# Attention and a gated feed-forward on one core: the mask and the identity loaded from SyncE's row, with the hand-written order of chunks 0 to 2 rewritten

## The chip, the core and the metric

The kernel runs on one core of a Trainium2 chip. TensorE (PE; its weight loads are listed as PEld), VectorE (DVE), ScalarE (ACT), GpSimd (POOL) and SyncE (SP) each run their own row of instructions in order and wait for each other by semaphores. The metric is the device time of one execution, in microseconds (us).

## The reference, cut to what matters

```python
# q, k, v: (4, 8, 768, 64); block 32, window 16
k_sum = k.reshape(B, H, 24, 32, D).max(axis=3)
v_sum = v.reshape(B, H, 24, 32, D).mean(axis=3)
scores_l = where(|i - j| < 16, q @ k.T / 8, -1e9)
scores_s = q @ k_sum.T / 8 + log(32)
a = softmax(concat(scores_l, scores_s))
x = a @ concat(v, v_sum)                      # heads side by side: (4, 768, 512)
h = relu(x @ w_in)                            # 512 -> 1024
gate = sigmoid(conv over 3 neighbours in the sequence, per feature, of h)
out = (h * gate) @ w_out                      # 1024 -> 512
```

Everything is float32.

## The kernel before, in words

The batch is worked off in 8 **chunks** of half a sequence (384 positions), and a chunk in 4 **head pairs**, so pairs are numbered n = 0 to 31. In a pair the scores of 6 query blocks of 64 are taken against 96 near keys and 24 block maxima.

The steps have short names, and a string `ORDER` lists them, in the order in which they are written, for chunks 0 to 2; each engine works off its own steps in that order. From chunk 3 on loops write the order, and they are not touched. The names, with n a pair, c a chunk, u a group of 128 of the 1024 features, fc one of the 8 parts of a weight:

- loads on SP: `R` transposed keys (400 KB), `Q` queries (192 KB), `T` transposed values (384 KB), `I`, `O` the raw words of w_in, w_out (512 KB a part), `V`, `K`, `M`, `C` values, keys, value means and convolution weights;
- attention: `ks` block maxima of the keys (DVE), `win` and `kb` copies of the near keys and of the maxima into one tile (POOL, or DVE with the letter v or for pair 0), `qk` scores (24 matmuls on PE), `mx` mask and row maximum (DVE, reads the mask), `ex` exponential (ACT), `sm`, `rc`, `nr` the row sum, its reciprocal and the scaling (ACT, DVE, POOL), `tr` transposes (PE, read the identity), `cp` the copy of these out of PSUM, `vs`, `pv`, `vm`, `vb` the means of the values, `av` the product with the values (PE), `xh`, `xl` its upper and lower part (ACT, DVE); `ed` copies two columns of the chunk before into a new chunk's xh and xl (DVE, L439);
- weights are put together from 64-bit words: `z` (ACT), `lo`, `st` (DVE, L179 and L185), then `hi` (ACT) and `wl` (POOL, L205), with i for w_in and o for w_out, and `locw`, `stcw` for the convolution weights;
- feed-forward: `f` first product of unit u, 4 parts of 3 matmuls (PE, L458), `re` relu, `ta`, `cv` the convolution, `th`, `mu` the gate (`mu` is DVE's L513 and is the last to read the PSUM tile of its unit), `gh`, `gl` upper and lower part, `g` second product (PE, L545);
- `w` n is n matmuls on a zero tile (L150): 12 stand ahead of the list (`WARM`).

Three PSUM tiles hold the units of the first product, so the first part of unit u can start when `mu` of unit u - 3 is done: `f0.3.0` after `mu0.0`, `f0.7.0` after `mu0.4`, `f1.1.0` after `mu0.6`, `f1.4.0` after `mu1.1`. The scores of pair n wait for all `mx` of pair n - 1. A text such as `sto0<nr5.1p` makes a step wait for another one, here DVE's `sto0` for POOL's `nr5.1`; in the code these are called shared port.

The mask (180 KB) and the identity (64 KB) are loaded ahead of the list, on ACT's own row, while SP begins with `R0 R1 Q0 R2`:

```python
        w(WARM)
        nc.scalar.dma_start(mask, mask8)
        nc.scalar.dma_start(ident, ident_in)
        for text in ORDER.split():
            run(text)
```

Of the kernel before, what the change touches and what calls it, by code (L numbers as in the profile page):

```python
# [48 lines left out]
mx0.0.1 kb4 Q3 mx0.0.2 zi1 kb2 mx0.1.0 loi1<kb2 ex0.0.2 mx0.1.1 ex0.1.0 sti1 V0 zi0 mx0.1.2 loi0
T1 ex0.0.1 w13 qk1 ex0.1.1 sti0 ex0.1.2 V1 mx1.0.0 win5<sti0 hii1 mx1.0.1 sm0 win3 hii0 mx1.0.2  # L50
rc0 Q4 mx1.1.0 ex1.0.1 nr0.0p mx1.1.1 T2 ex1.0.2 mx1.1.2 ex1.1.1 vs0 nr0.1p w9 tr0 ex1.1.0 qk2
ex1.1.2 wli0 ks3 T3 ex1.0.0 pv0 cp0a mx2.0.0 vm0 win6 w1 tr1 mx2.0.1 sm1 zi2 mx2.0.2 C rc1 kb3
ex2.0.1 mx2.1.0 kb5 V2 mx2.1.1 cp1a loi2<kb5 zi6 mx2.1.2 sti2 w6 qk3 ex2.0.2 I5 nr1.0v ex2.1.0
ex2.1.2 loi6 tr2 I4 vb0v ex2.1.1 ex2.0.0 sti6 av0 sm2 Q5 cp2a mx3.0.0 nr1.1p<sti6 rc2 mx3.0.1
hii2 vs1 V3 nr2.0p hii6 w1 tr3 mx3.0.2 cp3a pv1 nr2.1p T11 mx3.1.0 ex3.0.0 tr4 vm1v mx3.1.1 xh0
vb1 mx3.1.2 cp4a I3 xl0 w1 qk4 ex3.0.2 I7 wli2 vs2 ex3.1.0 av1 ex3.0.1 R8 mx4.0.0 ex3.1.1 vs3
wli1 pv2 ex3.1.2 tr5 vm2 sm3 mx4.0.1 xh1 pv3 f0.0.0 M4 mx4.0.2 ex4.0.1 win7 rc3 mx4.1.0 ex4.0.0
xl1 f0.1.0 vb2 zcw vm3 mx4.1.1 f0.0.1 cp5a mx4.1.2 Q6 ex4.1.1 locw<vb2 f0.2.0 nr3.0v ex4.1.2 O0
av2 stcw zi5 loi5 nr3.1v ex4.0.2 f0.1.1 sti5 xh2 tr6 zi4 wli6v qk5 cp6a loi4 ex4.1.0 tr7 sti4
hii5 mx5.0.0 vb3<sti4 sm4 xl2 cp7a hii4 mx5.0.1 rc4 kb7 w4 av3 mx5.0.2 ex5.0.0 wli4 mx5.1.0  # L60
ex5.0.1 vs11 f0.1.2 xh3 f0.0.2 ex5.0.2 mx5.1.1 nr4.0p O1 xl3 zi3 f0.2.1 Q7 mx5.1.2 ex5.1.0
loi3<nr4.0p f0.1.3 Q8 ex5.1.2 sti3 f0.0.3 M6 zi7 M7 kb6v tr8 loi7 re0.0 pv11 K8 f0.2.2 sti7 hii3
V4 ta0.0a ks8 f0.2.3 nr4.1p<sti7 M5 re0.1 qk6 wli3 cv0.0.0 cp8a ta0.1a tr9 cv0.0.2 re0.2 cv0.1.0
wli5 ex5.1.1 th0.0 mx6.0.0 cv0.1.2 sm5 cp9a hii7p mx6.0.1 th0.1 mu0.0 ta0.2a loo0<hii7p w9
f0.3.0 mx6.0.2 zo0 gh0.0p<loo0 rc5 mu0.1 f0.3.1 nr5.0p zo1 O2 mx6.1.0 cv0.2.0 f0.4.0 gh0.1 R10
gl0.0 mx6.1.1 tr10 ex6.0.2 ed4 f0.3.2 mx6.1.2 ex6.1.0 cv0.2.2 nr5.1p ex6.0.1 qk7 cp10v th0.2
sto0<nr5.1p ex6.1.2 f0.4.1 ex6.0.0 mx7.0.0 f0.3.3 loo1 ex6.1.1 f0.4.2 kb8v O4 sto1 vm11 re0.3
tr11 V5 hio0 mx7.0.1 gl0.1<sto1 f0.4.3 mu0.2 V6 sm6 ta0.3a av4 mx7.0.2 Q9 re0.4v wlo0 gh0.2 R9
rc6 mx7.1.0 ex7.0.0 f0.5.0 cv0.3.0 xh4 mx7.1.1 f0.5.1 nr6.0p cp11a cv0.3.2 ta0.4a g0.0 mx7.1.2
wli7 xl4 zo2 f0.5.2 cv0.4.0 ex7.0.1 tr12 ex7.1.1 ks10 nr6.1p f0.5.3 th0.3 qk8 cp12a loo2<nr6.1p  # L70
hio1 mu0.3 gl0.2<loo2 O3 tr13 ex7.1.2 cv0.4.2 K9 f0.6.0 re0.5 sto2<gl0.2 av5 th0.4 ta0.5a
mx8.0.0 wlo1<sto2 mu0.4 f0.6.1 gh0.3 mx8.0.1 ex7.0.2 f0.7.0 cv0.5.0 ex7.1.0 gl0.3 f0.6.2 mx8.0.2
zo4 cv0.5.2 f0.7.1 mx8.1.0 sm7 xh5 loo4 f0.6.3 th0.5 rc7 sto4 T8 f0.7.2 hio2 V7 mx8.1.1 g0.1
nr7.1p<sto4 cp13v re0.6 K10 ex8.0.0 mu0.5 f0.7.3 nr7.0p ta0.6a xl5 f1.0.0 ex8.1.1 wlo2 ks9 tr14
zo3 av6 cp14a cv0.6.0 kb9 hio4 g0.2 mx8.1.2 loo3<kb9 ex8.1.2 cv0.6.2 gh0.5p<loo3 O6 f1.0.1 re0.7
V8 sto3<gh0.5p tr15 th0.6 qk9 xh6 mu0.6 gl0.5<sto3 hio3 xl6 f1.1.0 cp15a vs8 wlo3 f1.0.2 ta0.7a
ex8.1.0 av7 mx9.0.0 O5 cv0.7.0 gh0.6 wlo4 Q10 ex8.0.1 f1.1.1 mx9.0.1 cv0.7.2 xh7 g0.3 mx9.0.2
th0.7 xl7 gl0.6 f1.1.2 ex8.0.2 mx9.1.0 mu0.7 zo6 f1.0.3 loo6 gh0.4 f1.2.0 mx9.1.1 T9 sto6 re1.0
f1.1.3 V9 ta1.0a kb10v pv8 mx9.1.2 f1.2.1 loo5 sm8 zo5 cv1.0.0 gl0.4<loo5 qk10 re1.1 rc8 O7
cv1.0.2 f1.2.2 ex9.1.2 Q11 sto5 th1.0 g0.4 vm8 nr8.0p<sto5 mu1.0 hio5 M8 f1.2.3 vs9 ta1.1a R11  # L80
wlo5 f1.3.0 gh0.7 Q12 tr16 cv1.1.0 hio6 M11 pv9 f1.3.1 re1.2 K11 nr8.1p cv1.1.2 g0.5 ex9.1.0 T10
mx10.0.0 cp16v gl0.7 th1.1 Q14 f1.3.2 mx10.0.1 ex9.0.0 mu1.1 tr17 vm9 ta1.2a f1.3.3 mx10.0.2 M9
gh1.0v cp17a f1.4.0 K12 cv1.2.0 wlo6<gh1.0v ex9.0.1 V11 av8 mx10.1.0 ex9.1.1 cv1.2.2 ex9.0.2
gl1.0 mx10.1.1 f1.4.1 th1.2 ks11 sm9 g0.6 re1.3 mu1.2 xh8 R17 f1.4.2 zo7 rc9 mx10.1.2 K13 f1.5.0
loo7 ex10.1.1 sto7 T17 f1.4.3 ta1.3a xl8 f1.5.1 kb11<sto7 ex10.0.2 nr9.0p hio7 cv1.3.0 qk11
ex10.1.2 wlo7 cv1.3.2 f1.5.2 K14 vs10 th1.3 tr18 f1.5.3 re1.4 nr9.1p mu1.3 ex10.1.0 T16 g0.7
mx11.0.0 cp18a V12 gh1.1p mx11.0.1 f1.6.0 M12 ob0 gh1.2v<gh1.1p gh1.3v tr19 mx11.0.2 kb12<gh1.3v
f1.6.1 mx11.1.0 ex10.0.1 re1.5v pv10 g1.0 ex10.0.0 gl1.3v f1.6.2 mx11.1.1 sm10p<gl1.3v ta1.4a
cp19v g1.1 ex11.0.0 rc10 cv1.4.0 ex11.1.1 nr10.0p f1.6.3 mx11.1.2 vm10 cv1.4.2 ex11.0.2 g1.2 M10
gl1.2 ex11.1.2 Q13 tr20 V10 qk12 nr10.1p ta1.5a ex11.1.0 g1.3 kb13 ex11.0.1 mx12.0.0 K15 gl1.1  # L90
cv1.5.0 th1.4 av9 mx12.0.1 cp20a mu1.4 sm11 g1.4 mx12.0.2 xh9 rc11 re1.6 xl9 tr21 g1.5 ta1.6a
cv1.5.2 cp21a mx12.1.0 f1.7.0 mx12.1.1 ex12.1.0 nr11.0v g1.6 th1.5 cv1.6.0 gh1.4p<nr11.0v
ex12.0.1 f1.7.1 kb14 cv1.6.2 tr22 g1.7 mu1.5 th1.6 mx12.1.2 gh1.5 av10 vs16 ex12.1.2 ex12.0.2
qk13 nr11.1v T18 cp22a xh10v gl1.5<nr11.1v M13 ob1 f2.0.0 mu1.6 R16 f1.7.2 mx13.0.0 K16 ex12.0.0
xl10 f2.1.0 Q17 ex12.1.1 mx13.0.1 vs17 f1.7.3 tr23 re1.7 mx13.0.2 g2.0 gl1.4v cp23a sm12v f2.0.1
ta1.7v pv17 rc12 g2.1 mx13.1.0 vm17 cv1.7.0 ex13.0.1 av11 kb15v gh1.6v nr12.0v g2.2 cv1.7.2
gl1.6<nr12.0v xh11 M15 ex13.1.0 Q15 mx13.1.1 f2.1.1 xl11 ex13.0.2 Q16 f2.0.2 nr12.1v th1.7 V15
mx13.1.2 f2.1.2 mu1.7 V13 f2.0.3 gh1.7p f2.2.0 re2.0 gl1.7 qk14 ex13.0.0 ex13.1.2 pv16 ex13.1.1
tr24 K17 f2.1.3 ta2.0a mx14.0.0 vm16v g2.3 sm13 mx14.0.1 re2.1 cp24v f2.2.1 ta2.1a mx14.0.2
cv2.0.0 tr25 ex14.0.2 rc13 g2.4 cv2.0.2 ex14.0.0 nr13.0p cp25a cv2.1.0 f2.2.2 th2.0 nr13.1p  # L100
mx14.1.0 g2.5 ex14.0.1 ks16 tr26 mx14.1.1 g2.6 cv2.1.2 ex14.1.1 mu2.0 av12 cp26a ex14.1.0
# [697 lines left out]
```

## Time and profile before

| | us |
|---|---|
| median of 3 runs | 378.69 (377.99 to 379.32) |
| the profiled execution, its own time | 379.11 |
| its span in the trace | 377.3 |
| PE busy | 368.1 |
| DVE busy | 255.2 |
| ACT busy | 236.6 |
| POOL busy | 140.7 |

The zero matmuls count as busy PE time. The views are the page, the windows (busy time of each engine in a stretch), the chain that ended last, the timeline of an engine, and the groups of instructions by line. Starts in the timeline of one engine can be closer together than the durations say, since instructions overlap by some tenths of a microsecond.

### The profile page before, as it was taken

How to read it: one execution, taken by the hardware profiler on the slowest of the kernel's cores; microseconds unless marked ns; L12 is line 12 of the kernel's file. 1: busy time of each engine (PE TensorE's matmuls, PEld its weight loads, DVE VectorE, ACT ScalarE, POOL GpSimd, SP SyncE). 2: the span in 40 equal slices, each digit the busy share in tenths (PEclk: the TensorE clock that was granted, in tenths of full speed). 3: DMA queues.
4: the chain of work that ended last, by engine and by line, in shares of the span. 5: the costliest groups of instructions: out<-in, count | busy, mean ns of one | idle time of the engine just before them, and what ended most of it. 6: DMA issues, size and time to landing. Idle time of an engine off the chain costs nothing.

```text
span 377.3 us, 8779 instructions
## 1 busy us (share of the span) xinstructions
PE 368.1 (98%) x3140; PEld 311.9 (83%) x3144; DVE 255.2 (68%) x801; ACT 236.6 (63%) x766; POOL 140.7 (37%) x182
## 2 busy tenths in 40 slices
...
GB/s 294 378 342 309 208 247 215 261 298 256 199 210 133 51 253 239 152 319 130 96 74 112 99 129 96 132 132 59 85 36 2 30 31 22 6 30 28 28 57 56
DMA packets 26859, 55.01 MB, mean 146 GB/s; under 512 B 3072, under 2 KB 11456, under 8 KB 26816
## 3 DMA queue, kind: packets, MB, share of 16 engines
...
q8 instruction: 25, 0.41, 0.5%
q14 instruction: 18, 0.15, 0.1%
...
## 4 chain that ended last, share of the span: by engine, by line
PE 84%; DVE 6%; POOL 5%; DMA 1%; issue 1%; ACT 1%; DVEq 0%; POOLq 0%; ACTq 0%
PE f L545 35%; PE f L458 32%; PE xp L416 6%; PE pt L402 5%; PE pq L345 5%; POOL win_lo L205 2%; PE pw L150 1%; DMA va<-vm 1%; POOL a L394 1%; DVE wu_i L185 1%; DVE a L359 1%; DVE wl_i L179 1%; POOL kw L300 1%; DVE t L513 0%; DVE t L495 0%
## 5 line engine op out<-in xcount | busy, mean ns | idle before, releaser
L526 POOL TENSOR_TENSOR glo<-t,ghi 128x383 fp32r<-128x383 f32 (+1 forms) x61 | 61.6, 1017 | 119.3 <-ACT ghi L523 93.4
L458 PE MATMUL f<-xh,win_hi 128*128 128x386 f32 (+1 forms) x256 | 91.6, 358 | 0.4 <-DVE t L513 0.2
L458 PE MATMUL f<-xh,win_lo 128*128 128x386 f32 (+1 forms) x256 | 86.4, 338 | 0.0
L458 PE MATMUL f<-xl,win_hi 128*128 128x386 f32 (+1 forms) x256 | 86.4, 338 | 0.0
L495 DVE SCALAR_TENSOR_TENSOR t<-f,cw,t 128x382 f32<-128x382 f32 (+3 forms) x128 | 78.4, 615 | 11.3 <-ACT t L484 8.8
L374 ACT ACTIVATE a<-a,nm 128x120 f32<-128x120 f32 x192 | 73.7, 386 | 10.8 <-DVE nm L359 9.1
L545 PE MATMUL f<-wout_hi,ghi 128*128 128x512 f32 x192 | 76.9, 401 | 0.0
L545 PE MATMUL f<-wout_lo,ghi 128*128 128x512 f32 x192 | 75.3, 392 | 0.0
L545 PE MATMUL f<-wout_hi,glo 128*128 128x512 f32 x192 | 75.0, 391 | 0.0
L458 PEld LDWEIGHTS f<-xh,win_hi 128*128 128x128 f32 x256 | 48.2, 188 | 6.3 <-DVE t L513 2.1
L506 ACT ACTIVATE t<-t 128x383 f32<-128x383 f32 (+1 forms) x64 | 32.4, 523 | 30.2 <-DVE t L495 29.6
L359 DVE CUSTOM_DVE_ANT_0 a<-pq,mask 128x120 f32<-128x120 f32 x192 | 45.8, 274 | 6.8 <-PE pt L402 3.8
L473 ACT ACTIVATE f<-f 128x386 f32<-128x386 f32 (+1 forms) x60 | 28.5, 475 | 34.6 <-PE f L458 34.4
L394 POOL TENSOR_TENSOR a<-a,sm 128x360 f32<-128x360 f32 x53 | 41.0, 789 | 24.7 <-DVE sm L390 8.6
L458 PEld LDWEIGHTS f<-xl,win_hi 128*128 128x128 f32 x256 | 48.3, 189 | 1.9
L458 PEld LDWEIGHTS f<-xh,win_lo 128*128 128x128 f32 x256 | 48.1, 188 | 0.0
L513 DVE SCALAR_TENSOR_TENSOR t<-t,f 128x383 f32<-128x383 f32 (+1 forms) x64 | 34.2, 551 | 15.9 <-ACT t L506 15.9
L486 DVE TENSOR_SCALAR t<-f,cw 128x385 f32<-128x385 f32 (+1 forms) x36 | 22.2, 616 | 31.6 <-ACT f L473 29.8
L545 PEld LDWEIGHTS f<-wout_hi,glo 128*128 128x128 f32 x192 | 36.0, 188 | 8.0
L545 PEld LDWEIGHTS f<-wout_hi,ghi 128*128 128x128 f32 x192 | 36.1, 188 | 5.8 <-issue 0.3
L545 PEld LDWEIGHTS f<-wout_lo,ghi 128*128 128x128 f32 x192 | 36.2, 188 | 4.5
L407 ACT COPY aT<-pt 120x384 f32<-120x384 f32 x56 | 26.5, 472 | 17.5 <-PE pt L402 17.4
...
## 6 DMA issues: line engine op xcount, KB each, us to landing
...
```

Of the source, the lines that this page charges most:

```text
L359: nc.vector.tensor_tensor_reduce(aa[n, h][:, i, :], pq[n][h][:, i * NK : (i + 1) * NK], mask[:, {(0, 0): 0, (1, 2): 2}.get((hf, i), 1), :] ...
L374: nc.scalar.activation(a, a, AF.Exp, bias=nm[n][:, h, i : i + 1], scale=-1.0, accum_out=sm[n][:, h, i : i + 1],)
L394: return engine[e].tensor_tensor(a, a, sm[n][:, h, :].unsqueeze(2).to_broadcast([P, 3, NK]), ALU.mult)
L407: return copy(aT[j][:NK, :], pt.pop(j)[:NK, : 3 * P])
L416: nc.tensor.matmul(xp[n][r, blk * QB : (blk + 1) * QB], v[:NK, blk, r], a[h][:NK, blk * QB : (blk + 1) * QB], start=True, stop=True,)
L458: nc.tensor.matmul(f1ps[c, u][:, :n], w[:, u, cc, :], x[:, cc, :n], start=(cc == 0 and m == 0), stop=(cc == NCC - 1 and m == 2),)
L473: nc.scalar.activation(h, h, AF.Relu)
L495: nc.vector.scalar_tensor_tensor(t[:, i0:i1], f1ps[c, u][:, hf + k - 1 + i0 : hf + k - 1 + i1], cw[:, u, k : k + 1], t[:, i0:i1], ALU.mult ...
L506: nc.scalar.activation(t, t, AF.Tanh, scale=0.5)
L513: return nc.vector.scalar_tensor_tensor(t, t, 1.0, h, ALU.add, ALU.mult)
L526: return engine[e].tensor_tensor(gate_rows("lo", c, u), conv.pop((c, u)), gate_rows("hi", c, u).bitcast(F32), ALU.subtract,)
L545: nc.tensor.matmul(f2ps[b, st], g[:, fc, ss], w[:, fc, :], start=(fc == 0 and m == 0), stop=(fc == NFC - 1 and m == 2),)
```

## The change

ACT's two loads ahead of the list are gone. A new step `X` issues them from SP: `X0`, the mask, stands as the fourth load behind `R0`, `Q0` and `R1`, and `X1`, the identity, as the tenth. The whole list of chunks 0 to 2 is written anew: which step stands where, and for some steps which engine does them.

```diff
-R0 R1 Q0 R2 I1 I0 Q1 ks0 R3 win0 T0 kb0 ks1 win1 Q2 qk0 I2 kb1 ks2 win2 I6 win4 mx0.0.0 ex0.0.0
...
+R0 Q0 R1 X0 I0 Q1 ks0 I1 win0 kb0 T0 qk0 R2 ks1 X1 Q2 kb1 R3 mx0.0.0 win4 V0 ex0.0.0 mx0.0.1
...
     def locw():
-        lower("cw", NFC * 3)
+        return lower("cw", NFC * 3)
...
+        "X": lambda i: nc.sync.dma_start(*((mask, mask8), (ident, ident_in))[i]),
...
         w(WARM)
-        nc.scalar.dma_start(mask, mask8)
-        nc.scalar.dma_start(ident, ident_in)
         for text in ORDER.split():
             run(text)
```

In the new list `locw` waits for nothing (before: `locw<vb2`), and POOL's `vb3` waits for it. On DVE's row ahead of `mu1.1` these steps stand now that didn't before (from POOL or ACT, or from behind `mu1.1`): `cp5`, `gh0.0`, `gl0.2`, `kb4`, `kb5`, `kb9`, `ks11`, `nr2.1`, `vb2`, `wli2`, `wli5`, `wlo4`; and these no longer stand there: `cp10`, `cp13`, `cp16`, `kb6`, `kb8`, `kb10`, two `mx10`, `nr1.0`, `nr3.0`, `nr3.1`, `re0.4`, `vb0`, `vm1`.

The order that comes of it, at three places. First, SP's row at the start of the program; kT are keys, raw_a words of w_in, raw_b there words of w_in or values. Before:

```order
L260 DMA kT_92<-kT 128x800
L260 DMA kT_94<-kT 128x800
L273 DMA q_96<-qT 128x384
L260 DMA kT_98<-kT 128x800
L223 DMA raw_a<-w_in 128x1024 x2
L273 DMA q_102<-qT 128x384
L260 DMA kT_106<-kT 128x800
L268 DMA raw_b<-vT 128x768
```

and now:

```order
L261 DMA kT_90<-kT 128x800
L274 DMA q_92<-qT 128x384
L261 DMA kT_94<-kT 128x800
L568 DMA mask<-mask 128x360
L224 DMA raw_a<-w_in 128x1024
L274 DMA q_98<-qT 128x384
L224 DMA raw_a<-w_in 128x1024
L269 DMA raw_b<-vT 128x768
L261 DMA kT_121<-kT 128x800
L568 DMA ident<-ident 128x128
```

The keys of pair 2 (kT_98 before, kT_121 now) went from the fourth load to the ninth. Second, DVE's row at its start, before:

```order
L145 MEMSET idle 128x256
L294 TENSOR_REDUCE ks_104<-kT_92 128x24
L300 COPY kw_108<-kT_92 128x6x96
L294 TENSOR_REDUCE ks_112<-kT_94 128x24
L294 TENSOR_REDUCE ks_134<-kT_98 128x24
L359 ISA a_0_142,nm_141<-pq_0_118,mask 128x120
```

and now:

```order
L146 MEMSET idle 128x256
L295 TENSOR_REDUCE ks_100<-kT_90 128x24
L301 COPY kw_103<-kT_90 128x6x96
L295 TENSOR_REDUCE ks_123<-kT_94 128x24
L360 ISA a_0_133,nm_132<-pq_0_107,mask 128x120
```

The maxima of pair 2 (`ks2`) no longer stand ahead of the first masked scores (`mx0.0.0`). Third, the two copies of `ed4` on DVE, which stood behind `mu0.1`, in the middle of the convolution of unit 2 (t_2), before:

```order
L495 SCALAR_TENSOR_TENSOR t_2_713<-f_0_2_500,cw,t_2_713 128x382
L359 ISA a_1_745,nm_702<-pq_1_673,mask 128x120
L359 ISA nm_702 128x1
L439 CAST xh_764<-xh_397 128x4x2
L439 CAST xl_765<-xl_398 128x4x2
```

and now:

```order
L186 SCALAR_TENSOR_TENSOR wu_i_612<-wu_i_612,wl_i_607 128x512
L440 CAST xh_629<-xh_367 128x4x2
L440 CAST xl_630<-xl_368 128x4x2
L180 TENSOR_SCALAR wl_i_636<-raw_a 128x512
L311 TENSOR_REDUCE vs_639<-vt_425 128x24
L186 SCALAR_TENSOR_TENSOR wu_i_622<-wu_i_622,wl_i_636 128x512
```

They stand now between `sti4` (wu_i_612) and `loi3` (wl_i_636), ahead of `mu0.0`. On POOL `nr4.0` must be done before `sti4` starts, and the next POOL step, `nr4.1`, waits for `loi3`.

## Rows read from the trace of the kernel before

**Rows 1.** Windows: stretch, its length, then busy us (instructions) of PE, PEld, DVE, ACT and POOL, PE's granted clock, DMA share, GB/s.

```profile
60.00:70.00 10.00, 10.00 (x114) 8.60 (x113) 9.87 (x30) 9.34 (x26) 7.55 (x9) 1.00 0.74 257
70.00:80.00 10.00, 10.00 (x95) 8.79 (x95) 9.72 (x30) 9.75 (x33) 7.04 (x7) 1.00 0.92 297
```

**Rows 2.** The chain that ended last, its pieces at 56 us (start, us, what): `mu0.4` and the first matmul of unit 7, `f0.7.0`.

```profile
56.13 0.48 DVE t L513
...
56.65 0.45 PE f L458
```

**Rows 3.** Timeline (start, us): three times DVE's `mu` and the first matmul of the unit that waits for its tile, `mu0.0` and `f0.3.0`, `mu0.6` and `f1.1.0`, `mu1.1` and `f1.4.0`; at 76.87 `f1.3.3`, which stands ahead of `f1.4.0` here.

```profile
40.88 0.55 DVE L513 SCALAR_TENSOR_TENSOR t<-t,f 128x383 f32<-128x383 f32 x1
...
41.49 0.44 PE L458 MATMUL f<-xh,win_hi 128*128 128x384 f32 x1 [0.19 <-DVE t L513]
...
64.22 0.55 DVE L513 SCALAR_TENSOR_TENSOR t<-t,f 128x383 f32<-128x383 f32 x1
...
64.97 0.45 PE L458 MATMUL f<-xh,win_hi 128*128 128x386 f32 x1
...
76.09 0.55 DVE L513 SCALAR_TENSOR_TENSOR t<-t,f 128x385 f32<-128x385 f32 x1
...
76.87 0.42 PE L458 MATMUL f<-xh,win_hi 128*128 128x386 f32 x1
...
77.48 0.34 PE L458 MATMUL f<-xh,win_hi 128*128 128x386 f32 x1
```

**Rows 4.** Timeline of the start (start, us; ACTq is an issue on ACT's row): the two loads, the 12 zero matmuls, `ks0`, `qk0`, `ks2` and `mx0.0.0`.

```profile
0.72 0.41 ACTq L603 DMA_DIRECT2D mask<-mask  x1
...
1.16 0.45 ACTq L604 DMA_DIRECT2D ident<-ident  x1
...
1.17 5.30 PE L150 MATMUL pw<-idle 128*128 128x512 bf16 x12 [1.17 <-DVE idle L145]
...
4.76 0.95 DVE L294 TENSOR_REDUCE ks<-kT 128x24 f32<-128x768 f32 x1 [3.65 <-DMA kT<-kT]
...
6.58 0.99 PE L345 MATMUL pq<-kw,q 64*64 64x120 f32 x24
...
7.46 0.95 DVE L294 TENSOR_REDUCE ks<-kT 128x24 f32<-128x768 f32 x1 [0.53 <-DMA kT<-kT]
...
8.34 0.27 DVE L359 CUSTOM_DVE_ANT_0 a<-pq,mask 128x120 f32<-128x120 f32 x1
```

**Rows 5.** Windows of the start, columns as in rows 1 (the last is GB/s of the loads).

```profile
0.00:3.00 3.00, 1.83 (x5) 0.74 (x6) 0.27 (x1) 1.28 (x1) 0.19 (x4) 1.00 0.29 54
3.00:4.00 1.00, 1.00 (x4) 0.31 (x3) 0.00 (x0) 0.00 (x0) 0.00 (x0) 1.00 0.97 378
4.00:5.00 1.00, 1.00 (x4) 0.32 (x3) 0.24 (x1) 0.00 (x0) 0.00 (x0) 1.00 1.06 409
5.00:11.00 6.00, 5.77 (x47) 2.60 (x49) 5.40 (x19) 2.35 (x9) 3.15 (x7) 1.00 1.04 412
```

**Rows 6.** Line L439, all four runs of each copy of `ed` (ns: least, median, most), and then the timeline around `ed4`, of DVE and of POOL.

```profile
L439 DVE CAST xh<-xh x4: 172/297/760, 43.5 to 274.8; 128x8 fp32r<-128x8 f32 x4
L439 DVE CAST xl<-xl x4: 159/172/832, 44.1 to 274.7; 128x8 fp32r<-128x8 f32 x4
...
43.47 0.76 DVE L439 CAST xh<-xh 128x8 fp32r<-128x8 f32 x1
44.14 0.83 DVE L439 CAST xl<-xl 128x8 fp32r<-128x8 f32 x1
...
43.18 1.02 POOL L526 TENSOR_TENSOR glo<-t,ghi 128x383 fp32r<-128x383 f32 x1
44.16 0.79 POOL L394 TENSOR_TENSOR a<-a,sm 128x360 f32<-128x360 f32 x1
```

**Rows 7.** Timeline around `locw` (L179, 24 elements a partition), the like-sized `stcw` (L185), and POOL's `vb2`.

```profile
27.27 0.66 DVE L179 TENSOR_SCALAR wl_cw<-cw_words 128x24 uint32<-128x24 uint32 x1
...
28.28 0.17 DVE L185 SCALAR_TENSOR_TENSOR cw<-cw,wl_cw 128x24 uint32<-128x24 uint32 x1
...
27.07 0.82 POOL L332 COPY va<-vm 24x768 f32<-24x768 f32 x1
```

**Rows 8.** Groups by line and shape on DVE up to 80 us (count, busy us, mean ns of one): `ks`, `cp`, `nr`, `wl`, `kb`, `re`, `vb`, `gh`, `vm`.

```profile
L294 DVE TENSOR_REDUCE ks<-kT 128x24 f32<-128x768 f32 x8 | 7.6, 947 | 4.2 <-DMA kT<-kT 4.2
...
L407 DVE COPY aT<-pt 120x384 f32<-120x384 f32 x3 | 1.6, 548 | 0.0
L394 DVE TENSOR_TENSOR a<-a,sm 128x360 f32<-128x360 f32 x3 | 1.6, 528 | 0.0
...
L205 DVE TENSOR_TENSOR win_lo<-wu_i,win_hi 128x512 fp32r<-128x512 f32 x1 | 0.7, 699 | 0.0
L304 DVE COPY kw<-ks 128x144 f32<-128x144 f32 x3 | 0.7, 226 | 0.0
...
L475 DVE TENSOR_SCALAR f<-f 128x384 f32<-128x384 f32 x1 | 0.6, 559 | 0.0
L332 DVE COPY va<-vm 24x768 f32<-24x768 f32 x1 | 0.6, 553 | 0.0
...
L523 DVE CAST ghi<-t 128x385 fp32r<-128x385 f32 x1 | 0.4, 356 | 0.0
L328 DVE TENSOR_SCALAR vm<-pv 24x128 f32<-24x128 f32 x1 | 0.3, 274 | 0.0
```

137 lines of the change are left out of this document (69 added, 68 removed).

## The prediction

> **What bounds the kernel now.** I read the windows first, then the chain that ended last, then the timeline at the places that it names. From 60 to 80 us PE is busy for all of both windows, and DVE for 9.87 and 9.72 of 10 [rows 1]. The chain leaves DVE for PE at 56.65 and is nearly all PE from there: `mu0.4` ends on DVE at 56.13 + 0.48 = 56.61, and `f0.7.0` starts 0.04 later [rows 2]. So the time is set by how early PE gets into its unbroken stretch. What comes after is PE's own work, which the change doesn't alter: the same matmuls stand in the list, and one zero matmul more. Every microsecond that DVE's row is earlier at the gates of PE is one off the end, as long as PE needs DVE there. The gates show how near the two run: `mu0.0` ends at 41.43 and `f0.3.0` starts at 41.49; `mu0.6` ends at 64.77 and `f1.1.0` starts at 64.97; `mu1.1` ends at 76.64 and `f1.4.0` starts at 77.48 [rows 3]. DVE is the engine to count, and its slack is 0.06, 0.2 and 0.84.
>
> **The loads at the start.** In the trace the keys of pair 0 let `ks0` start at 4.76, with the mask, the identity and the next keys in flight beside them [rows 4]. By then the loads had moved 3 x 54 + 378 + 0.76 x 409 = 850 KB [rows 5], of which 410 KB (128 x 800 x 4 bytes) are the keys of pair 0. Without the mask's and the identity's 250 KB, 600 KB have to move, which is reached at 4.15. So `ks0` comes about 0.6 earlier. **Little of that reaches PE:** the 12 zero matmuls hold PE from 1.17 to 6.47 and `qk0` starts at 6.58 [rows 4], and these 12 are still there. `qk0` then ends at 7.57, as before, and the mask's load, the fourth, has long landed: the first four loads are 1.2 MB, moved by about 5.6 [rows 5]. What is gained is that `ks2`, which waited for its keys until 7.46 and took 0.95, no longer stands ahead of `mx0.0.0` [rows 4]. That step can start at about 7.7 in place of 8.34, so ACT begins its exponentials 0.65 earlier. For DVE it is no gain: `ks2` is still to be done. Its net is -0.65 + 0.87 (the start-to-start time of `ks2` and `mx0.0.0`, 8.34 - 7.46 [rows 4]), **+0.2**. Bounds: -0.6 if `ks2` falls into a stretch where DVE would wait anyway, +0.9 if `mx0.0.0` doesn't move. `ks2`'s keys, now the ninth load, have some 2.8 MB ahead of them and land at about 10.6 to 11 at 412 GB/s [rows 5]; DVE comes to `ks2` at about 12.4, after `vs0` and half of pair 1, so that load is covered with over a microsecond to spare.
>
> **ed4.** Both copies of `ed4` move 8 elements a partition, and took 0.76 and 0.83; other runs of the same line took 0.16 to 0.17 [rows 6]. The first ends at 44.23, just as POOL's `gl0.0` ends at 44.20, and the second at 44.97, as POOL's `nr5.1` ends at 44.95 [rows 6]. A DVE copy waits here until POOL's instruction is over. In the new list `ed4` stands behind `sti4`, which itself waits for POOL's `nr4.0`, and POOL's next step waits for `loi3`, which stands behind `ed4`. POOL is idle there, and the two copies should take 2 x 0.17. Term: 0.34 - 1.59 = **-1.2**. Bounds: 0 if POOL runs there after all, -1.25.
>
> **locw.** It works on 24 elements a partition and took 0.66, ending at 27.93 with POOL's `vb2` at 27.89; `stcw`, of the same size, took 0.17 [rows 7]. Now `vb3` waits for `locw`, and the POOL step ahead of that, `win7`, ends before `vb2`, which is on DVE itself and waits for it. Term: 0.17 - 0.66 = **-0.5**; bounds 0 and -0.5.
>
> **DVE's other steps, up to mu1.1.** Gone from the row by then: three `nr` at 0.53, three `cp` at 0.55, three `kb` at 0.23, `re` 0.56, `vb` 0.55, `vm` 0.27 [rows 8] and two `mx` at 0.27 [rows 4], 5.8 in all. New: three `wl` at 0.70, `ks11` 0.95, `cp` 0.55, `vb` 0.55, `nr` 0.53, three `kb` at 0.23, `gh` 0.36 [rows 8], and `gl0.2`, which no row of this stretch shows on DVE: it subtracts one SBUF tile from another as `wl` does and on about as many elements as `nr`, so 0.5 to 0.7; I take `nr`'s 0.53 for its shape. That is 6.2. Net **+0.4**; since the instructions overlap by about 0.1 each, 0.3 to 0.6.
>
> **The sum.** DVE at `mu1.1`: +0.2 - 1.2 - 0.5 + 0.4 = -1.1, so it ends at 75.5. `f1.3.3` no longer stands ahead of `f1.4.0`, so PE, if it never waited, would want `mu1.1` earlier than before by the 77.48 - 76.87 = 0.61 of that part [rows 3]. Of the slack of 0.84 some 0.2 stay. The end can therefore come 1.1 + 0.2 = 1.3 earlier before DVE binds at `f1.4.0`. At `f1.1.0` the slack is 0.2 and DVE's terms are the same to 0.1, so 1.2 or so. I take the smaller, **1.2**. The profiled execution has 379.11 of its own; by the sum the same execution would have 377.9. The median lies 0.42 below that execution, so 378.69 - 1.2 = **377.5**. All other waits of DVE are taken as equal in both lists; that is the weakest part, since every wait in the first 60 us is a new one.
>
> **A rule that speaks against it.** The Trainium skill, "DMA: Bandwidth & Descriptors", section "Issuing engines are not separate DMA queues", says that transfers issued from several engines interleave on the same 16 DMA engines, and that spreading the issues saves only the issuer's sequencer time. By that the move costs SP what ACT did beside it and buys no bandwidth. The second half agrees with the rows as far as they go, since the windows from 4 to 11 us move 409 to 412 GB/s [rows 5], but the order of service is another matter.
>
> **Rivals.** *Larger gain.* If ACT's earlier start also takes away DVE's waits for ACT in the first pairs, and the extra 0.4 falls into waits, then the terms are -0.65 - 1.2 - 0.5 = -2.35 and the time 376.3. For: ACT runs ahead of DVE's need by more. Against: at `f1.4.0` and later DVE carries more steps, and its slack there was under 1.
>
> *No change.* `ed4` meets a POOL instruction again, or PE finds the next late engine at the same gates. Then +0.2 - 0.5 + 0.4 = 0.1 and 378.8; with half of `ed4`'s term 378.1. Against: the two waits that keep POOL away stand in the list.
>
> *Loads late by SP's issues.* The two issues took 0.41 and 0.45 on ACT [rows 4] and now stand in SP's row. If the loads were limited by SP, everything behind would come 0.86 later, and 0.86 - 1.2 gives 378.3. Against: the windows from 4 to 11 us are at the same 409 to 412 GB/s whatever SP issues [rows 5], so the transfers are behind, not the issues.
>
> *Slower.* A new wait stands at pair 3. Its scores (`qk3`) now follow nine zero matmuls and `tr2` on PE, `tr2` needs `nr1.0`, which went from DVE (0.53 [rows 8]) to POOL behind `wli0` and `win3`. The DVE steps that filled this stretch, the weights of parts 2 and 6, went behind `mx3.1.2`. So DVE has nothing but `vs1` to do until `qk3` is there; by the same durations I count about 1.2 of idle time on DVE for it, as much as DVE's small waits there before, which is why I set it at nothing. Should the chain `zi1`, `sti1`, `wli0`, `win3`, `nr1.0`, `tr2`, `qk3` end later than I count, each microsecond goes to DVE and to the end. From 1.2 more the change is no gain, from 2.4 more it is slower by over 0.3%; at 2.7 more the time is 380.2. For: work passes from engine to engine four times in that chain, and each hand-over can be late. Against: by the same durations every step in it has its other inputs early.
>
> **Chances.** The forecast case (376.9 to 378.1) has 0.45, the larger gain 0.17, no change 0.15, the late loads 0.06, the slower one 0.17. What a measurement of this kernel can tell from no change is about 0.3%, or 1.1, so the line lies at 377.55 and cuts the forecast case nearly in half: a bit over half of it, 0.27, and the larger gain make **0.44** for faster; the rest of it, no change, the late loads and a little of the slower case 0.40; slower 0.16. The range takes in the larger gain and half of the slower case: 375.9 to 379.7.
>
> **What would show it.** `mx0.0.0` at about 7.7 with `qk0` still at 6.5; both copies of `ed4` under 0.35 and `locw` at 0.2; `f0.3.0` at 40.3, earlier by 1 or more; `mu1.1` at about 75.5; PE without gaps from then on. I would be wrong if DVE stands idle over 2 us ahead of `mx3.0.0`, if `ed4` is long again, if `mx0.0.0` comes after 8.3, or if PE waits again between 60 and 100 us, where the new list gives DVE more to do.

## The result and the profile after

| | before | after |
|---|---|---|
| median (us) | 379.00 (4 runs, 377.99 to 379.33) | 383.51 (4 runs, 382.93 to 383.78) |
| profiled execution: own time, span | 379.11, 377.3 | 383.29, 381.5 |

The ratio is 1.0121, with a 95% interval of 1.0103 to 1.0139: the change makes the kernel 4.5 us slower. The forecast was 377.5, the range ended at 379.7.

The places named in the prediction come first. They are the timeline rows of after (start, us) that answer to [rows 3, 4, 6, 7]: `ks0`, `qk0`, `ks1`, `mx0.0.0`, `locw`, the two copies of `ed4`, `mu0.0` with the first matmul of `f0.3.0`, and `mu1.1`.

```profile
3.79 0.95 DVE L295 TENSOR_REDUCE ks<-kT 128x24 f32<-128x768 f32 x1 [2.68 <-DMA kT<-kT]
...
6.23 0.85 PE L346 MATMUL pq<-kw,q 64*64 64x120 f32 x24
...
6.38 0.95 DVE L295 TENSOR_REDUCE ks<-kT 128x24 f32<-128x768 f32 x1 [1.26 <-DMA kT<-kT]
...
7.33 0.28 DVE L360 CUSTOM_DVE_ANT_0 a<-pq,mask 128x120 f32<-128x120 f32 x1
...
31.09 0.17 DVE L180 TENSOR_SCALAR wl_cw<-cw_words 128x24 uint32<-128x24 uint32 x1
...
35.58 0.17 DVE L440 CAST xh<-xh 128x8 fp32r<-128x8 f32 x1
...
35.65 0.17 DVE L440 CAST xl<-xl 128x8 fp32r<-128x8 f32 x1
...
40.25 0.55 DVE L514 SCALAR_TENSOR_TENSOR t<-t,f 128x383 f32<-128x383 f32 x1
...
40.85 0.44 PE L459 MATMUL f<-xh,win_hi 128*128 128x384 f32 x1 [0.52 <-DVE t L514]
...
74.53 0.55 DVE L514 SCALAR_TENSOR_TENSOR t<-t,f 128x385 f32<-128x385 f32 x1
```

All but `ks1` (5.99 before) are earlier or shorter than before. `mx0.0.0` starts at 7.33 (8.34 before), `locw` and both copies of `ed4` take 0.17 each, and `mu1.1` ends at 75.08 against 76.64. So the front is not where the time went. The waits view of TensorE in after (us in total, times, longest) shows one wait that stands out:

```profile
PE f L546 <- ACT ob L556: 3.9, 1, 3.9
...
PE pt L403 <- POOL a L395: 0.8, 2, 0.6
```

Where is it? The timeline of after around 147 us: the first and the last matmul of `f3.0` (the first product of chunk 3), ScalarE's `th2.7` and `th2.6` (one row), `ob4`, the first of the nine second products that TensorE wants next, and the transposes behind them.

```profile
145.00 0.42 PE L459 MATMUL f<-xh,win_hi 128*128 128x386 f32 x1
...
147.03 0.34 PE L459 MATMUL f<-xh,win_lo 128*128 128x386 f32 x1
...
149.62 1.11 ACT L507 ACTIVATE t<-t 128x383 f32<-128x383 f32 x2 [1.73 <-DVE t L496]
...
150.63 0.58 ACT L556 ACTIVATE ob<-f 128x512 f32<-128x512 f32 x1
...
151.26 0.79 PE L546 MATMUL f<-wout_hi,ghi 128*128 128x512 f32 x1 [3.89 <-ACT ob L556]
...
155.27 0.84 PE L403 MATMUL pt<-ident,a 128*120 128x128 f32 x3
```

TensorE is through with `f3.0` at 147.4 and can't go on. Its next matmuls write the only PSUM tile of the second product. That tile still holds output tile 4, and `ob4`, the copy on ScalarE that frees it, starts at 150.63. `ob4` waits for no data by then: the last product of that tile was over at 143.2. It stands behind `th2.7` and `th2.6` on ScalarE's row, and these wait for VectorE's convolution (1.73 `<-DVE t L496`). In the kernel before, `ob4` runs ahead of `f3.0`, and the products follow it with no wait (`ob4`, the first matmul of `f3.0`, the first product, the transposes behind the nine):

```profile
145.93 0.59 ACT L555 ACTIVATE ob<-f 128x512 f32<-128x512 f32 x1
...
147.27 0.42 PE L458 MATMUL f<-xh,win_hi 128*128 128x386 f32 x1
...
149.48 0.40 PE L545 MATMUL f<-wout_hi,ghi 128*128 128x512 f32 x1
...
151.54 0.49 PE L402 MATMUL pt<-ident,a 128*120 128x128 f32 x3
```

In the list the move is plain to see:

```diff
-f2.7.3 th2.5 f2.6.1 re2.7 mu2.5 ob4 ta2.7v f2.6.2 ...
+f2.7.3 mu2.5 re2.7 gh2.5p f2.6.2 ta2.7a ... cv2.6.2 th2.7 th2.6 mu2.6
+mu2.7 gh2.7p gl2.7v<gh2.7p ob4 gh2.6v gl2.6<gh2.6v
```

The wait is paid twice. Windows of after, columns as in [rows 1]:

```profile
149.00:151.00 2.00, 0.00 (x0) 0.00 (x0) 1.88 (x5) 1.32 (x3) 0.00 (x0) 0.59 0.00 0
151.00:153.00 2.00, 1.74 (x4) 1.45 (x5) 1.93 (x5) 0.74 (x2) 0.50 (x1) 0.50 0.34 131
153.00:155.00 2.00, 2.00 (x6) 1.52 (x6) 2.00 (x4) 0.00 (x0) 1.00 (x1) 0.50 0.00 0
155.00:157.00 2.00, 2.00 (x33) 1.39 (x33) 1.25 (x2) 0.99 (x2) 1.24 (x2) 0.70 0.91 262
157.00:159.00 2.00, 2.00 (x35) 1.84 (x34) 1.43 (x10) 1.12 (x4) 0.07 (x1) 1.00 0.78 220
```

The granted clock falls within the wait, and behind it it is 0.50, the lower of TensorE's two levels (1.2 GHz), and it is back at 1.00 only from 157 on. The nine products take 155.27 - 151.26 = 4.01; in the kernel before the same nine took 2.06, from 149.48 to 151.54.

**The account.** The first matmul of `f3.0` is a point at which TensorE has the same work behind it in all these kernels, zero matmuls apart, and in the traces the same 1754 matmuls still to do. Before reaches it at 147.27, after at 145.00: 2.27 ahead. From there to the end of the span it is 230.0 before and 236.5 after, 6.5 more: 3.89 for the wait, 1.95 for the nine products, 0.40 for the transposes, value products and scores right behind them (2.74 in place of 2.34), and 0.2 that these rows do not place. 6.5 - 2.27 = 4.2, the difference of the two spans. The 2.27 is of one pair of traces; by the medians it is 6.5 - 4.5 = 2.0.

### The profile page after: what moved, and what is told of

Its sections match the earlier page's. It is cut to its first block, busy times and chain, and to the rows that moved or that the text cites. A ratio compares the mean times of both kernels' runs of the same rounds, so it can differ in the third digit from the quotient of the medians.

```text
span 381.5 us, 8770 instructions
## 1 busy us (share of the span) xinstructions
PE 369.5 (97%) x3141; PEld 313.4 (82%) x3145; DVE 256.9 (67%) x807; ACT 237.7 (62%) x765; POOL 131.4 (34%) x177
## 4 chain that ended last, share of the span: by engine, by line
PE 83%; DMA 7%; DVE 5%; POOL 2%; issue 2%; SPq 1%; ACT 1%; POOLq 0%; ACTq 0%
PE f L546 35%; PE f L459 31%; PE xp L417 6%; PE pt L403 5%; PE pq L346 5%; DMA raw_b<-vT 4%; DMA raw_a<-w_in 3%; DVE t L496 1%; POOL a L395 1%; DVE a L360 1%; DVE wu_o L186 1%; DVE wl_o L180 0%; DVE wu_i L186 0%; DVE t L514 0%; PE pv L320 0%
## 5 line engine op out<-in xcount | busy, mean ns | idle before, releaser
L527 POOL TENSOR_TENSOR glo<-t,ghi 128x385 fp32r<-128x385 f32 (+1 forms) x57 | 57.4, 1016 | 123.2 <-ACT ghi L524 103.3
L459 PE MATMUL f<-xh,win_hi 128*128 128x384 f32 (+1 forms) x256 | 91.5, 358 | 0.8 <-DVE t L514 0.8
L459 PE MATMUL f<-xl,win_hi 128*128 128x384 f32 (+1 forms) x256 | 86.7, 339 | 0.0
L459 PE MATMUL f<-xh,win_lo 128*128 128x384 f32 (+1 forms) x256 | 86.5, 338 | 0.0
L496 DVE SCALAR_TENSOR_TENSOR t<-f,cw,t 128x382 f32<-128x382 f32 (+3 forms) x128 | 78.2, 614 | 9.9 <-ACT t L485 7.5
L395 POOL TENSOR_TENSOR a<-a,sm 128x360 f32<-128x360 f32 x54 | 41.8, 789 | 34.2 <-DVE sm L391 12.2
L474 ACT ACTIVATE f<-f 128x386 f32<-128x386 f32 (+1 forms) x57 | 27.1, 475 | 31.6 <-PE f L459 31.2
L487 DVE TENSOR_SCALAR t<-f,cw 128x385 f32<-128x385 f32 (+1 forms) x39 | 24.1, 618 | 32.9 <-ACT f L474 31.2
L408 ACT COPY aT<-pt 120x384 f32<-120x384 f32 x62 | 29.4, 474 | 17.7 <-PE pt L403 17.3
```

The costliest lines, as they stand in the source:

```text
L395: return engine[e].tensor_tensor(a, a, sm[n][:, h, :].unsqueeze(2).to_broadcast([P, 3, NK]), ALU.mult)
L408: return copy(aT[j][:NK, :], pt.pop(j)[:NK, : 3 * P])
L459: nc.tensor.matmul(f1ps[c, u][:, :n], w[:, u, cc, :], x[:, cc, :n], start=(cc == 0 and m == 0), stop=(cc == NCC - 1 and m == 2),)
L474: nc.scalar.activation(h, h, AF.Relu)
L487: nc.vector.tensor_scalar(t, h, cw[:, u, 1:2], 1.0, ALU.mult, ALU.mult)
L496: nc.vector.scalar_tensor_tensor(t[:, i0:i1], f1ps[c, u][:, hf + k - 1 + i0 : hf + k - 1 + i1], cw[:, u, k : k + 1], t[:, i0:i1], ALU.mult ...
```

## The experiments

The theory (A): the front's gain is real, and `ob4`'s place loses it and more. The rivals: the heavier row of VectorE or the loads through SyncE cost the time (B), or the clock falls for a reason of its own (C).

**1. `ob4` back behind `re2.7`, all else as changed.**

```diff
-f2.7.3 mu2.5 re2.7 gh2.5p ... gl2.7v<gh2.7p ob4 gh2.6v
+f2.7.3 mu2.5 re2.7 ob4 gh2.5p ... gl2.7v<gh2.7p gh2.6v
```

> The changed kernel with one step moved in the list: ob4, ScalarE's copy of the fifth output tile out of PSUM, from the end of the list to right behind re2.7, where it stood before. Theory A (the front is ahead by some 2.3 us, and the loss is a TensorE wait of 3.9 for ob4 at 147 us with a lowered clock behind it): the wait is gone, the granted clock is 1.00 in every window from 140 to 170, the first matmul of f3.0 is still at about 145.0, and the time is 376.7 to 377.5, some 2 below the kernel before. Rival B (the heavier VectorE row or the loads through SyncE cost the time, and the wait only shows it): TensorE waits for something else in the same place and the time is 380 or more. Rival C (the clock falls for another reason than the wait): the wait of 3.9 is gone but the window 150 to 155 is still at 0.5, and the time is about 379.5.

Measured: 377.83 (12 runs, 376.35 to 378.99), ratio 0.9976 [0.9964, 0.9987], 5.7 less than with `ob4` at the end and 0.9 less than before. Timeline: `ob4`, the first matmul of `f3.0`, VectorE's first step of the convolution of unit 7 (`cv2.7.0`), the first of the products, and the first matmul of `f3.1`.

```profile
143.08 0.60 ACT L556 ACTIVATE ob<-f 128x512 f32<-128x512 f32 x1
...
143.90 0.42 PE L459 MATMUL f<-xh,win_hi 128*128 128x386 f32 x1
...
144.70 0.61 DVE L496 SCALAR_TENSOR_TENSOR t<-f,cw,t 128x382 f32<-128x382 f32 x1 [0.28 <-ACT t L485]
...
146.11 0.39 PE L546 MATMUL f<-wout_hi,ghi 128*128 128x512 f32 x1
...
151.12 0.45 PE L459 MATMUL f<-xh,win_hi 128*128 128x386 f32 x1 [0.38 <-DVE t L514]
```

The products follow `f3.0` with no wait, and the clock is 1.00 up to 170. B and C fall as causes of the loss: with one step moved in the list, of the 6.5 behind `f3.0` 0.7 is left. Of that, 0.38 is a wait of TensorE for VectorE's `mu2.6`, in the last row: `ob4` and the issue of its store hold ScalarE's row from 143.08 to 144.04, just ahead of `ta2.7`, and VectorE waits 0.28 for `ta2.7`. The trace is of the fastest of the 12 executions (376.35). The median is 0.3 above what A gave; experiments 7 to 10 look for that.

**2. The reverse: the kernel before, `ob4` late.**

```diff
-re2.7 mu2.5 ob4 ta2.7v ... mu2.6 th2.7 gh2.6p
+re2.7 mu2.5 ta2.7v ... mu2.6 th2.7 ob4 gh2.6p
```

> The kernel before with one step moved: ob4 from right behind re2.7 to behind th2.7, so that ScalarE gives up the output tile last. Theory A: in the trace before, th2.6 and th2.7 are over at 152.5, so ob4 ends at about 153.1; TensorE, which wanted the tile at 149.5, waits 3.5 there, the granted clock falls to 0.5 in the windows behind, and the time is 383.5 to 385.5. Rivals B and C (ob4's place has no part in it): 378.5 to 379.5.

Measured: 383.68 (383.12 to 384.11), ratio 1.0130 [1.0114, 1.0147]. Timeline (`ob4` and the first of the nine products), then windows:

```profile
152.05 0.58 ACT L555 ACTIVATE ob<-f 128x512 f32<-128x512 f32 x1
...
152.68 0.55 PE L545 MATMUL f<-wout_hi,ghi 128*128 128x512 f32 x1 [3.39 <-ACT ob L555]
```

```profile
153.00:155.00 2.00, 2.00 (x6) 1.60 (x5) 1.86 (x5) 0.51 (x1) 1.40 (x2) 0.50 0.69 139
155.00:157.00 2.00, 2.00 (x11) 1.35 (x12) 1.96 (x3) 0.04 (x1) 0.12 (x1) 0.65 0.73 249
```

Nearly the same wait and the same fall of the clock in the old list, with the old loads: `ob4`'s place alone makes a loss of 4.9 (by the ratio; 5.1 from `f3.0` to the end in the trace).

**3. `ob4` late, but ahead of `th2.7`.** Two kernels were to give TensorE a wait of 1.0 and of 2.5, by marks like `sto0<nr5.1p`:

```diff
-cv2.7.2 vm18 cv2.6.2 th2.7 ... gl2.7v<gh2.7p ob4 gh2.6v
+cv2.7.2 vm18 ob4<ta2.6v cv2.6.2 th2.7 ... gl2.7v<gh2.7p gh2.6v
```

(the second with `ob4<cv2.6.0`).

> The changed kernel with ob4 ahead of th2.7 on ScalarE and made to wait for VectorE's ta2.6, so that TensorE waits about 1.0 for the output tile in place of 0 (ob4 behind re2.7) or 3.9 (as changed). If the lowered clock comes with any such wait: the window behind it at 0.5 for some us, and the time 1.0 + 2 above that with ob4 behind re2.7, near 381. If a short wait leaves the clock alone: granted clock 1.00 throughout and 1.0 above, near 378.8. If ob4 plays no part: 377.8.

> The same with ob4 made to wait for VectorE's cv2.6.0 instead, so that TensorE waits about 2.5. If the clock falls behind a wait of this length: near 382.4 with a window at 0.5 (2.5 + 2.1 above the kernel with ob4 behind re2.7). If it does not: near 380.3 with the clock at 1.00. The two runs together with 0 and 3.9 give the price of the wait and of the clock apart.

Measured: 377.36 (376.70 to 377.83), ratio 0.9969 [0.9959, 0.9979], and 377.55 (one run of six at 381.88), ratio 0.9990 [0.9956, 1.0025]. The marks did not hold ScalarE: in the code a mark is taken up only for a step that returns its instruction, and `ob` returns none, so the edit only changes `ob4`'s place. In the timeline of the first, `ob4` runs ahead of the step `ta2.6` that it was to follow, and the products start right at the end of `f3.0`:

```profile
145.41 0.57 ACT L556 ACTIVATE ob<-f 128x512 f32<-128x512 f32 x1
...
147.09 0.61 DVE L487 TENSOR_SCALAR t<-f,cw 128x383 f32<-128x383 f32 x1
...
147.50 0.39 PE L546 MATMUL f<-wout_hi,ghi 128*128 128x512 f32 x1
```

So these tell nothing of a short wait. They show that `ob4` may stand far down the list as long as the step behind which ScalarE waits comes after it. Here `ta2.7` comes ahead of `ob4`, TensorE's wait of 0.38 for `mu2.6` is gone, and both traces need 230.2 from `f3.0` on where experiment 1 needs 230.7; the medians of 1 and 3 don't part beyond their intervals.

**4. The loads alone.** The kernel before with nothing moved but the loads, once with the queries of pair 0 second as in the change, once with the keys of pair 1 second as before.

```diff
-R0 R1 Q0 R2 I1 I0 Q1 ks0 R3
+R0 Q0 R1 X0 R2 I1 I0 Q1 X1 ks0 R3     (first kernel)
+R0 R1 Q0 X0 R2 I1 I0 Q1 X1 ks0 R3     (second kernel)
```

> The kernel before with nothing but the loads moved: mask fourth and identity ninth in SyncE's row, queries of pair 0 second, no loads on ScalarE; the hand-written order of the other steps as before, so ks2 still stands ahead of mx0.0.0. By the prediction's working: ks0 0.6 to 0.9 earlier, qk0 bound by the zero matmuls and ks2 by its keys as before, so mx0.0.0 at 8.2 to 8.5 and the time within 0.5 of 379.0. Rival (SyncE pays for the two issues, 0.86): 379.9. Rival (the move itself is the gain): mx0.0.0 at 7.4 and 378.0 or less.

> The kernel before with nothing but the mask and the identity moved to SyncE's row, behind the first two keys and the first queries (keys 0, keys 1, queries 0, mask); unlike the earlier run of the loads alone, the keys of pair 1 stay ahead of the queries. If it was the keys of pair 1, 1.0 later behind the queries, that cost 0.65 there: ks1 at 5.3 or less, mx0.0.0 at 8.3 or less, time 378.0 to 378.6. If the issues on SyncE or the mask ahead of the keys of pair 2 cost it: ks2 at 8.4 and mx0.0.0 at 9.3 again, 379.2.

Measured: 379.50 (378.29 to 380.45), ratio 1.0019 [1.0007, 1.0031], and 378.86 (378.14 to 380.39, one of twelve at 1242), ratio 1.0014 [1.0000, 1.0027]. Timeline of the first, `ks0`, `ks1` and `mx0.0.0`:

```profile
3.66 0.95 DVE L294 TENSOR_REDUCE ks<-kT 128x24 f32<-128x768 f32 x1 [2.55 <-DMA kT<-kT]
...
6.98 0.95 DVE L294 TENSOR_REDUCE ks<-kT 128x24 f32<-128x768 f32 x1 [2.00 <-DMA kT<-kT]
...
9.29 0.27 DVE L359 CUSTOM_DVE_ANT_0 a<-pq,mask 128x120 f32<-128x120 f32 x1
```

`ks0` is 1.1 earlier, where 0.6 was counted, but `ks1` starts 1.0 later (5.99 before), and `mx0.0.0` comes at 9.29 in place of 8.34. In the second kernel `ks1` is at 5.10 and `mx0.0.0` at 8.38, as before; so the late `ks1` goes with the queries standing second. That the second median still lies 0.5 up, at the edge of its interval, is not explained by these steps, and the two kernels' intervals overlap. The windows of the loads, in GB/s:

| mask and identity issued by | kernel | second load | `ks1` starts | 2 to 3 us | 4 to 5 | 0 to 7 |
|---|---|---|---|---|---|---|
| ScalarE | before | keys | 5.99 | 125 | 409 | 254 |
| ScalarE | changed, loads back (5) | queries | 6.82 | 124 | 390 | 248 |
| SyncE | loads alone, first | queries | 6.98 | 329 | 216 | 217 |
| SyncE | loads alone, second | keys | 5.10 | 330 | 304 | 256 |
| SyncE | after | queries | 6.38 | 291 | 296 | 223 |
| SyncE | `ob4` back (1) | queries | 5.21 | 272 | 382 | 271 |

With all the loads on SyncE's row, ten traces move 272 to 330 GB/s from 2 to 3 us and 191 to 382 from 4 to 5; four traces with two issuers move 107 to 155 and 390 to 415. Over the first 7 us the ten have 214 to 271 and the four 248 to 261. After and experiment 1 issue the same loads in the same order at the start and have 223 and 271, so a price of the single issuer is not shown. Nor do SyncE's issues limit the loads: by 4.0 us SyncE in after has issued 2.4 MB, of which 0.7 MB have moved. The Trainium skill, "DMA: Bandwidth & Descriptors", section "Issuing engines are not separate DMA queues", was cited in the prediction for "buys no bandwidth": issuing from several engines saves only the time of the issuing sequencer. The sums over 7 us do not speak against it.

**5. The new list with the loads back on ScalarE** (and `ob4` behind `re2.7`).

```diff
+nc.scalar.dma_start(mask, mask8)
+nc.scalar.dma_start(ident, ident_in)
-R0 Q0 R1 X0 I0 Q1 ks0 ... ks1 X1 Q2
+R0 Q0 R1 I0 Q1 ks0 ... ks1 Q2
```

> The changed kernel with ob4 behind re2.7 and, besides, the mask and the identity back on ScalarE ahead of the list: the new order without the move of the loads. If the new order is what brings the front ahead and the loads matter by the keys of pair 1 alone (ks1 waited for these until 6.38, and 250 KB beside them are 0.6 us): mx0.0.0 at 7.9, and the time 0 to 0.6 above that of the same kernel with the loads on SyncE. If the loads are what brings the front ahead: 1.5 or more above it.

Measured: 378.39 (377.45 to 381.31), ratio 0.9999 [0.9977, 1.0020]; `mx0.0.0` at 7.69. The median is 0.6 above that of experiment 1, the upper end of what the theory gave, and the intervals overlap; by the ratio alone nothing of the gain over before is left. So the new order brings `mx0.0.0` ahead by itself, but whether the loads' place has a part in the time is open. Eight of the twelve executions lie from 377.45 to 378.60, four from 379.79 to 381.31, and the trace is of one of these (380.04).

**6. `ed4` alone, in the kernel before.**

```diff
-ex6.0.2 ed4 f0.3.2 ... loi3<nr4.0p f0.1.3
+ex6.0.2 f0.3.2 ... loi3<nr4.0p ed4 f0.1.3
```

> The kernel before with nothing but the two copies of ed4 moved from behind mu0.1 to right behind loi3, where POOL stands idle until nr4.1. By the prediction's working each copy takes 0.17 in place of 0.76 and 0.83, and VectorE is 1.2 ahead from there: f0.4.0 and the later gates of TensorE up to 1.2 earlier, time 377.7 to 378.3. Rival (a wait for something else takes the place: TensorE's qk7 waited 0.53 at 45.2, and the gates behind have other limits): copies short, but the time within 0.4 of 378.9. Rival (the copies meet another POOL instruction): still 0.7 to 0.8 each, and no gain.

Measured: 378.00 (377.75 to 378.33), ratio 0.9981 [0.9971, 0.9991], 0.7 less by the ratio. Timeline: POOL is idle between the two scalings, `nr4.0` and `nr4.1`, and the copies take 0.17:

```profile
34.10 0.80 POOL L394 TENSOR_TENSOR a<-a,sm 128x360 f32<-128x360 f32 x1
...
35.28 0.17 DVE L439 CAST xh<-xh 128x8 fp32r<-128x8 f32 x1
...
35.35 0.17 DVE L439 CAST xl<-xl 128x8 fp32r<-128x8 f32 x1
...
37.58 0.79 POOL L394 TENSOR_TENSOR a<-a,sm 128x360 f32<-128x360 f32 x1 [2.68 <-DVE wu_i L185]
```

The first matmul of `f3.0` is at 145.85, 1.42 earlier than before, in that trace; the ratio gives half of it. The trace of before is one of its longer executions (379.11, where the median beside this run is 378.52), so the pair of traces shows too much.

**7 to 10. Where the rest of the gain stays.** The kernel of experiment 1 spreads over 2.6 us, and in the trace of experiment 5 TensorE waited 2.79 at 61.56 while VectorE waited 2.22 for words of w_out. Four edits of the loads at 45 to 62 us, all with `ob4` behind `re2.7`:

```diff
 (7) the values of pairs 6 and 7 ahead of O3
-mu0.3 O3 ... O4 th0.4 sto2 av5 V6 sm7 re0.5 V7
+mu0.3 V6 V7 O3 ... O4 th0.4 sto2 av5 sm7 re0.5
 (8) parts 3 and 4 of w_out exchanged
-mu0.3 O3 ... O4 th0.4
+mu0.3 O4 ... O3 th0.4
 (9) as (8), and the keys of pair 1 ahead of the queries
-R0 Q0 R1 X0
+R0 R1 Q0 X0
 (10) the keys of pair 10 earlier
-V5 mx7.0.2 ... mx8.0.1 R10 ks9
+V5 R10 mx7.0.2 ... mx8.0.1 ks9
```

> The changed kernel with ob4 behind re2.7 and the value loads of pairs 6 and 7 (V6, V7) ahead of O3 in SyncE's row, where they were issued at 53.3 behind O4, one pair ahead of their use; in the kernel before V6 and V7 were issued well ahead. If these loads are what TensorE waits for ahead of the value products at 53 to 61 (0.4 in one run, 2.8 in the one with the loads on ScalarE): these waits are gone, the spread of the runs shrinks from 2.6 (376.35 to 378.99) and the median is 377.0 to 377.5. If not: 377.8 with the same spread. Rival: the parts of w_out come later behind them and VectorE waits; 378.5.

> The changed kernel with ob4 behind re2.7, and the loads of the parts 3 and 4 of w_out exchanged in the list, since loo4 reads its part some 5 us ahead of loo3; the new list loads O4 only when loo2 has freed its buffer, 3.8 to 6 us ahead of loo4. If the late part O4 is what makes the runs of the kernel with ob4 back spread from 376.35 to 378.99 (VectorE waited 2.22 for w_out in the trace with the loads on ScalarE, 1.27 in the one with V6 and V7 early, 0 in the one with ob4 back): no wait of VectorE for w_out at 54 to 60, spread under 1.5, median 376.6 to 377.3. Rival (the spread comes from the first keys, ks1 at 5.2 to 6.8): spread and median as with ob4 back, 377.6 to 378.

> The same with the keys of pair 1 ahead of the queries of pair 0 in SyncE's row, as in the kernel before. ks1 waited for these keys 1.26 in the trace of the changed kernel. If VectorE's start counts to the end: ks1 right behind ks0, mx0.0.0 bound by qk0 at 6.2 to 7.3, and 0.3 to 0.8 less than with the exchange alone. If qk0 is late for its queries instead, or the start is taken up by later waits: within 0.3.

> The changed kernel with ob4 behind re2.7, and the load of the keys of pair 10 (R10, 400 KB) moved from behind V6, V7 and K9, where it is issued at 54.7, to right behind V5, where it can be issued at about 47 and VectorE needs it only at 64. Four traces of the new list show TensorE waiting at 53 to 61 for one of the loads issued at 50 to 55 (w_out words or the values of pair 7), 0.4 in the fastest and 1.7 to 3.2 in the slow ones, while the DMA share is 0.92 to 1.02 from 54 to 62. If the crowd at 54 to 62 is what delays these loads: no TensorE wait over 0.5 there, first matmul of f3.0 at 143.9 to 145.3 in the trace, median 376.6 to 377.3, spread under 1.6. Rival (R10's own bytes at 47 to 51 only push O3 and O4 back, as the values of pairs 6 and 7 did): 379 or more. If neither: 377.8 and a spread of 2.6 as with ob4 back.

Measured: (7) 381.52 (378.72 to 383.58), 1.0070 [1.0048, 1.0092]; (8) 378.10 (377.17 to 379.00), 0.9989 [0.9978, 1.0000]; (9) 378.31 (377.01 to 380.85), 0.9997 [0.9977, 1.0018]; (10) 380.31 (378.75 to 381.49), 1.0036 [1.0018, 1.0055]. None is better than experiment 1, and two are worse by 3.7 and 2.5. Timeline of (7), `loo4` and the value products of pair 7:

```profile
59.03 0.43 DVE L180 TENSOR_SCALAR wl_o<-wo 128x512 uint32<-128x512 uint32 x1 [1.27 <-DMA wo<-w_out]
...
60.19 0.92 PE L417 MATMUL xp<-aT,va 120*64 120x64 f32 x24 [1.75 <-DVE xl L447]
```

and of (10), the issues of `R10` and `O4`, then `loo4` and the value products:

```profile
48.31 0.42 SPq L261 DMA_DIRECT2D kT<-kT  x1
...
53.98 0.33 SPq L229 DMA_DIRECT2D wo<-w_out  x1
...
59.96 0.43 DVE L180 TENSOR_SCALAR wl_o<-wo 128x512 uint32<-128x512 uint32 x1 [1.92 <-DMA wo<-w_out]
...
61.32 0.92 PE L417 MATMUL xp<-aT,va 120*64 120x64 f32 x24 [2.50 <-DMA va<-v_win]
```

In (10) `O4` is issued at 53.98, VectorE waits 1.92 for it until 59.96, and the values of pair 7, issued behind it, hold TensorE until 61.32. That the early load makes these words late is not shown by the trace alone: in experiment 5, where no load there was moved, `O4` was issued at 54.04 and VectorE waited 2.22 for it until 60.29, while in experiment 1 it was issued at 52.90 and there at 56.67. What the executions show is how often it costs. In (7) the mean granted clock is 0.991 to 0.996 in the seven longest of eleven executions (380.99 to 383.58) and 1.00 in the other four (378.72 to 380.34); in (10) it is 0.995 or 0.996 in five of ten (380.75 and up), and at least 0.999 in the others (378.75 to 379.88). So more than the waits is lost there: in about half of the executions or more the clock falls too.

The theory fell for (7), (8) and (10). The rival beside (7) had the wait right and its price too low (378.5), the one beside (10) came true (379 or more), and (9) stayed within 0.3 of (8), with `mx0.0.0` at 6.80, bound by `qk0`. The DMA share is 0.94 to 1.05 from 48 to 60 in (10), and both loads put ahead cost more than they gave. That the late loads make the spread of experiment 1 is not shown: the traces of long executions (380.04 in 5, 379.76 in 9) have TensorE waiting 2.79 and 3.16 at 61, those of short ones (376.35 in 1, 377.17 in 8) 0.37 and 0.38, which fits it, but (8) narrowed the spread only to 1.8, without a lower median.

**All traces in one table.** Start of `f3.0`, span, and the difference:

| kernel | `f3.0` | span | from there |
|---|---|---|---|
| before | 147.27 | 377.3 | 230.0 |
| after | 145.00 | 381.5 | 236.5 |
| 1, `ob4` back | 143.90 | 374.6 | 230.7 |
| 2, `ob4` late in before | 146.93 | 382.0 | 235.1 |
| 3, `ob4` ahead of `th2.7` | 145.28, 146.01 | 375.5, 376.2 | 230.2, 230.2 |
| 4, loads alone | 147.61, 146.28 | 377.7, 376.4 | 230.1, 230.1 |
| 5, loads back on ScalarE | 147.62 | 378.2 | 230.6 |
| 6, `ed4` alone | 145.85 | 375.9 | 230.0 |
| 7, 8, 9, 10 | 146.28, 144.69, 147.30, 148.94 | 376.9, 375.4, 378.0, 379.6 | 230.6, 230.7, 230.7, 230.7 |

From `f3.0` on all kernels need 230.0 to 230.7, except the two in which `ob4` is late.

## Why the prediction was wrong

**The step that failed** is in its first part: "What comes after is PE's own work, which the change doesn't alter." The matmuls are the same, but what lets them start is not. The list ends with chunk 2, and its last steps on ScalarE hold what chunk 3 waits for: TensorE waited 3.89 for `ob4`, and 6.5 us went from `f3.0` on. The prediction followed one kind of gate to the end, `mu` and the three PSUM tiles of the first product, and never asked who frees the single tile of the second. `ob4`'s move was in the diff, in the last lines of the list, and it has no term. Of the sentence "All other waits of DVE are taken as equal" the prediction said that it was its weakest part; the wait that counted was not VectorE's. None of the four signs by which it said that it would be wrong is in the trace of after; all four lie ahead of 100 us.

**The sum was right in sign and a little small.** VectorE at `mu1.1`: -1.1 forecast, 75.08 - 76.64 = -1.56 measured. `ed4` gave 1.25 and `locw` 0.49, as counted. For `mx0.0.0` 7.7 was given, and it came at 7.33, though `ks1` waited 1.26 for its keys, which no term had. `f0.3.0` came at 40.85 in place of 40.3. With `ob4` where it was, the kernel takes 377.8 or 377.4 (experiments 1 and 3), around the forecast of 377.5, and the range failed for want of a rival with `ob4`'s mechanism. That 377.5 fits the change without that step is in part luck: `f0.3.0` gained 0.64 where 1.2 was forecast, `mu1.1` gained more than forecast, what the list changes between `mu1.1` and `f3.0` has no term, and experiment 1 lost 0.7 again behind `f3.0`. (One rival's sum is off by 0.1, half of `ed4`'s term gives 378.2; nothing rests on it.)

**The loads** were set at +0.2 on VectorE, with bounds of -0.6 and +0.9. Alone in the old list they cost 0.7 at the end [0.3, 1.2] with the queries second. What no term had is the place of the second keys: with the queries ahead of them `ks1` started at 6.12 to 6.98 in eight of nine traces, with the keys second at 5.10 to 5.99 in five. The working also took the rates of [rows 5] for the new issue order; from 4 to 7 us after moved 296 GB/s and experiment 1, with the same loads, 390, where before moved 412.

**ed4** as a term on VectorE was right. That all of it reaches the end was not: 0.7 [0.3, 1.1] of 1.2.

**The slower rival** named the chain into `qk3`. `mx3.0.0` waited 1.24, as counted, and nothing came of it; slower came by another road, outside the windows in which the prediction said PE might wait (60 to 100 us).
